# First weights in halves on two queues, an earlier place for block 1's statistics, a later one for two blocks of x

## The chip, the cores and the metric

The kernel runs on one core of a Trainium2 chip. Its engines work side by side, each through its own instructions in order: TensorE (PE, matrix products, with its weight loads as PEld), VectorE (DVE), ScalarE (ACT), GpSimd (POOL) and SyncE (SP). SP, ACT and POOL also issue DMA transfers, which sixteen DMA engines carry out. The metric is the device time of one execution in microseconds, lower is better.

## The reference

The input x has 2048 rows (tokens) of 512 columns in bfloat16. It is normalised by row, and two branches work on the result:

```python
xn = _layernorm(x, axis=-1)
# branch A: a diagonal complex state-space model along the 2048 tokens, 512 states
Bu = xn @ B_bar.T;  h[t] = Lam_bar * h[t-1] + Bu[t];  yA = 2 * (h @ C.T).real + xn * Dskip
# branch B: a gated MLP with 1792 hidden columns
yB = (silu(xn @ w1) * (xn @ w3)) @ w2
out = x + yA + yB
```

w1 and w3 are 512x1792 and w2 is 1792x512. The output is bfloat16.

## The kernel before

**Blocks.** The tokens are taken in 4 blocks of 512 (`TBLK`), each of 4 chunks of 128 rows. One tile `x_all` holds all of x, `x_blk[b]` is a block of it. For a block the kernel forms the statistics of each row (`ln_stats`, DVE), scales the rows (`xn`), transposes them (`xnT`: the 512 columns as four tiles of 128 partitions, the "depth"), multiplies with w1 and w3 (`glu`, hidden columns in 14 groups `f` of 128), forms the inputs of the state model (`bu`), scans along the tokens on DVE, and multiplies gates and states with w2 and C in seven products of sums (`y_fast`, for pairs of chunks).

**The start.** Block 0 is done by chunks, so that work can begin with the first 128 rows. x's chunks 0 and 1 are loaded in column halves, left on SP's queue and right on ACT's. Then come chunk 3 on ACT's queue (L167), chunk 2 on SP's (L168), and columns 0 to 255 and 256 to 511 of w1 and w3 (`load_w`, L169 and L170), 256 KB each, all four depths in one transfer. All of these go out before any compute instruction of SP and ACT. ACT then loads its function table (L199). PE warms up on ones (`keep_busy`, L196), transposes chunks 0 and 1 (L243) and multiplies them with the first two hidden groups in `quarter` (L619). The first `quarter` works in two depth parts: w1 with depths 0 and 1, w1 with depths 2 and 3, then w3 in the same way, eight matmuls for each of w1 and w3. The transposes of chunks 2 and 3 and the third hidden group (`quarter(0, (2,))`, columns 256 to 383) follow in PE's row. On DVE the statistics of chunks 2 and 3 stand one after the other, and behind both the scaling of chunk 2 and of chunk 3 (L224).

**Queues.** `bulk_loads` (called after the first statistics) sends the other columns of w1 and w3, x of block 1, and transposed loads of B and C over SP. `late_loads` sends w2, the row Dskip, and x of blocks 2 (by chunks) and 3 over SP. Each transfer of SP or ACT uses one of eight semaphores in turn, and the built program makes its issue wait until the transfer that used the same one eight places earlier has landed.

**The order of DVE's background work.** The order of all engines is written out by hand. Beside the products, a list `bg` of tasks is worked off: each has a cost in us, and `bg.fill()` emits tasks while DVE's planned time is less than 1.7 us (`LEAD`) ahead of PE's. `bg.flush(key)` emits all up to the last task of that key. At the start of block 0 the list holds `table_angles(2, 2)` (L376 to L380: the angles of two of the four state tiles, of which ACT makes sines and cosines later), then block 1's four statistics and the two POOL steps to its scale `rstd` (`ln1a`: L219, L220, L254, L255), then block 1's scaling and transposes (`ln1b`: L224, L247), `late_loads` and `params_w`. `ssm_tasks(0)` adds the state work of block 0 in halves: `pre` (rotation), `scans`, `post` (rotation back, whose last step is a POOL transfer that adds into `act`, L527).

**Block 2 and 3's x.** ACT forms their statistics by itself (`ln_scalar_engine`: L274, L280), emitted through `sin_step`, between evacuations of block 1's products.

Of the kernel before, what the change touches and what calls it, by code (L numbers as in the profile page):

```python
# [17 lines left out]
P = 128  # L18
# [45 lines left out]
def kernel(  # L64
# [17 lines left out]
    nc = tc.nc  # L82
# [26 lines left out]
    xv = A_x[0].rearrange("(c p) d -> p c d", p=P)  # L109
# [15 lines left out]
    w1_sb = const.tile([P, NDT, F], BF16, name="w1_sb")  # L125
    w3_sb = const.tile([P, NDT, F], BF16, name="w3_sb")
# [23 lines left out]
    x_all = xpool.tile([P, NBLK, CPB, D], BF16, name="x_blk")  # L150
    x_blk = [x_all[:, i] for i in range(NBLK)]
    w1v = B_w1.rearrange("(t p) f -> p t f", p=P)
    w3v = B_w3.rearrange("(t p) f -> p t f", p=P)

    def load_w(f0, f1, eng1=nc.sync, eng3=nc.sync):
        eng1.dma_start(out=w1_sb[:, :, f0:f1], in_=w1v[:, :, f0:f1])
        eng3.dma_start(out=w3_sb[:, :, f0:f1], in_=w3v[:, :, f0:f1])

    def load_x(b, parts=1):
        n = CPB // parts  # L160
        for i in range(0, CPB, n):
            nc.sync.dma_start(out=x_blk[b][:, i:i + n, :], in_=xv[:, b * CPB + i:b * CPB + i + n, :])

    for c in range(2):
        for eng, dsl in ((nc.sync, slice(0, D // 2)), (nc.scalar, slice(D // 2, D))):
            eng.dma_start(out=x_blk[0][:, c, dsl], in_=xv[:, c, dsl])  # L166
    nc.scalar.dma_start(out=x_blk[0][:, 3, :], in_=xv[:, 3, :])  # L167
    nc.sync.dma_start(out=x_blk[0][:, 2, :], in_=xv[:, 2, :])  # L168
    load_w(0, 2 * P)  # L169
    load_w(2 * P, 4 * P)  # L170

    def bulk_loads():
# [9 lines left out]
    def late_loads():  # L182
        nc.sync.dma_start(out=w2_sb, in_=B_w2.rearrange("(t p) d -> p t d", p=P))
        nc.sync.dma_start(out=dskip_row, in_=A_Dskip.partition_broadcast(P))
        load_x(2, 4)
        load_x(3)

# [23 lines left out]
    bg = Filler(LEAD)  # L211
# [37 lines left out]
    def ln_tasks_vector(b):  # L249
        csl = slice(b * CPB, (b + 1) * CPB)  # L250

        def finish_stats():
            vpe = lnp.tile([P, CPB], FP32, name="vpe")
            nc.gpsimd.tensor_scalar(out=vpe, in0=mv_all[:, csl, 1], scalar1=LN_EPS, scalar2=None, op0=ALU.add)  # L254
            nc.gpsimd.tensor_tensor(out=rstd_all[:, csl], in0=vpe, in1=mhalf, op=ALU.pow)  # L255

        def apply(cl):
            if cl == 0:
                ln_alloc(b)
            ln_apply(b, cl)  # L260
            ln_transpose(b, cl)

        first = [(0.85, lambda cl=cl: ln_stats(b, cl)) for cl in range(CPB)] + [(0.0, finish_stats)]
        second = [(0.4, lambda cl=cl: apply(cl)) for cl in range(CPB)]
        return first, second
# [74 lines left out]
    def sin_step(until=None):  # L340
        while sins and (until is None or until not in sins_done):
            key, fn = sins.popleft()
            fn()
            sins_done.add(key)
            if until is None:
                break
# [23 lines left out]
    def table_angles(pt, n=1):  # L370
        if pt + n > 3:
            sin_step((pt + n - 4, 0))
        slots = scratch[:, 0:2 * NPT * 2 * TBLK].bitcast(FP32).rearrange("p (h i t) -> p h i t", h=2, t=TBLK)
        ang, rnd = slots[:, 0, pt:pt + n, :], slots[:, 1, pt:pt + n, :]
        for i in range(n):
            nc.vector.tensor_scalar(out=ang[:, i, :], in0=iota_f, scalar1=turn[:, pt + i:pt + i + 1], scalar2=None,  # L376
                                    op0=ALU.mult)
        nc.vector.tensor_scalar(out=rnd, in0=ang, scalar1=MAGIC, scalar2=None, op0=ALU.add)
        nc.vector.scalar_tensor_tensor(out=ang, in0=rnd, scalar=MAGIC, in1=ang, op0=ALU.subtract, op1=ALU.subtract)
        nc.vector.tensor_scalar(out=rnd.bitcast(DT.int32), in0=ang.bitcast(DT.int32), scalar1=0x7FFFFFFF, scalar2=None,  # L380
                                op0=ALU.bitwise_and)
        for k in range(pt, pt + n):
            for i, (src, bias, scale) in enumerate(((rnd, halfpi, -TWO_PI), (ang, 0.0, -TWO_PI))):
                sins.append(((k, i), lambda k=k, i=i, src=src[:, k - pt, :], bias=bias, scale=scale: nc.scalar.activation(
                    out=tabe[:, k, i, :], in_=src, func=ACT.Sin, bias=bias, scale=scale)))
# [76 lines left out]
    def ssm_tasks(b, posts_last=False, between=(), middle=(), late=()):  # L462
# [76 lines left out]
        def add(*fns):  # L539
            for fn in fns:  # L540
                bg.add(0.0 if fn in transfers else 1.2 if fn in scans0 or fn in scans1 else 1.16, fn,
                       ("scan", b) if fn in scans0 else ("post", b) if fn in post0 else ("ssm", b))

        if b == 0:
            add(*pre0, *scans0, *post0, *pre1, *scans1, *post1)
            return
        add(*pre0)
        for t in middle:
# [32 lines left out]
    def glu(b):  # L581
# [76 lines left out]
        for f in range(f0, NFT):  # L658
            if f == AHEAD[b]:
                if b == 0:  # L660
                    ssm_tasks(0)
                if b == 2:
                    sin_step(("squares", 3, CPB - 1))
                    bg.flush(("bu", 0))
                    steps.extend(bu_fast(b, 0))
                    second = lambda: bu_fast(b, 1)
                else:
                    bu(b)
# [497 lines left out]

    ln_alloc(0)
    ln1a, ln1b = ln_tasks_vector(1)
    bg.add(3.6, lambda: table_angles(2, 2))
    for t in ln1a:  # L1170
        bg.add(*t)
    for t in ln1b:
        bg.add(*t, ("ln", 1))
    bg.add(0.0, late_loads, ("ln", 1))
    bg.add(0.2, params_w)
    gate = glu(0)
# [33 lines left out]
    def keep_ends(b):  # L1210
# [3 lines left out]
        nc.vector.tensor_copy(out=ends, in_=act(b)[:, CPB - 1].rearrange("p (h k) t -> p h k t", h=2)[:, :, NFH:NK, P - 1])  # L1214

    ssm_tasks(1, between=[(0.2, lambda: keep_ends(0))])
    gate = glu(1)
    gate()
# [6 lines left out]
    for cl, o in held:  # L1225
        nc.sync.dma_start(out=ov[:, cl, :], in_=o)
    bg.add(*difference(1))
    ssm_tasks(2, between=res_list(3), late=[(0.2, lambda: keep_ends(1)), *row_sums(2, *pairs[2]), *column_sums(3)])
    bg.first(bu_sums(2))
    gate = glu(2)  # L1230
# [52 lines left out]
```

## Time and profile before

| | us |
|---|---|
| median of 3 runs (lowest to highest) | 200.94 (200.86 to 201.03) |
| span of the profiled execution | 199.5 |
| PE busy, matmuls | 195.6 |
| DVE busy | 181.8 |
| ACT busy | 135.0 |
| POOL busy | 51.5 |

The profiled execution's span runs from its first to its last instruction; its share of the measured time outside the span is some 1.4 us if it took as long as the median. Rows of the profile name the line of the kernel, the engine, the operation, the tile written and the tiles read. A time in brackets is how long the engine stood idle before the instruction, with what ended the idle time. "SPq" and "ACTq" are DMA issues in SP's and ACT's row; a transfer's time to landing counts from the start of its issue. In the table of stretches each engine has its busy time in us and its number of instructions; the last three columns are the granted clock of TensorE, the mean busy share of the DMA engines and GB/s.

### The profile page before, as it was taken

How to read it: one execution, taken by the hardware profiler on the slowest of the kernel's cores; microseconds unless marked ns; L12 is line 12 of the kernel's file. 1: busy time of each engine (PE TensorE's matmuls, PEld its weight loads, DVE VectorE, ACT ScalarE, POOL GpSimd, SP SyncE). 2: the span in 40 equal slices, each digit the busy share in tenths (PEclk: the TensorE clock that was granted, in tenths of full speed). 3: DMA queues.
4: the chain of work that ended last, by engine and by line, in shares of the span. 5: the costliest groups of instructions: out<-in, count | busy, mean ns of one | idle time of the engine just before them, and what ended most of it. 6: DMA issues, size and time to landing. Idle time of an engine off the chain costs nothing.

```text
span 199.5 us, 3700 instructions
## 1 busy us (share of the span) xinstructions
PE 195.6 (98%) x1401; PEld 130.7 (65%) x1401; DVE 181.8 (91%) x254; ACT 135.0 (68%) x281; POOL 51.5 (26%) x75
## 2 busy tenths in 40 slices
PE   8999999999999999999999999999999999999994
PEld 2774444444444488866555468888566678888893
DVE  3689699999999999989999997999999999999972
ACT  4699897699999996968998684362588783111220
POOL 7180289700411134041202305040021303310000
PEclk9999999999999999999999999999999999999999
DMA  4999996991497054730997455838137732941111
GB/s 138 326 277 200 302 186 124 343 273 23 69 181 141 0 105 82 135 105 0 156 148 119 89 92 98 172 83 132 53 59 129 149 56 52 174 92 36 53 44 40
DMA packets 32258, 25.12 MB, mean 126 GB/s; under 512 B 16240, under 2 KB 29936, under 8 KB 32240
## 3 DMA queue, kind: packets, MB, share of 16 engines
q0 software_dynamic: 6128, 11.38, 33.5%
q1 hardware_dynamic: 25536, 13.21, 26.8%
q10 hardware_dynamic: 576, 0.30, 0.5%
q8 instruction: 11, 0.18, 0.4%
q14 instruction: 7, 0.06, 0.1%
HBM read 7.74 MB, written 2.10 MB: 49 GB/s over the span
## 4 chain that ended last, share of the span: by engine, by line
PE 95%; DMA 2%; SPq 1%; issue 0%; DVE 0%
PE gu_ps L587 34%; PE gu_ps L1054 17%; PE y_ps L1054 10%; PE gu_ps L848 7%; PE bu_ps L1054 7%; PE bu_ps L454 3%; PE y_ps L454 3%; PE y_ps L869 3%; PE y_ps L780 3%; DMA w_sb<-in_B_w_dram 2%; PE gu_ps L619 2%; PE gu_ps L780 2%; PE bu_ps L869 1%; PE bu_ps L780 1%; PE bu_ps L619 1%; SPq L166 0%
## 5 line engine op out<-in xcount | busy, mean ns | idle before, releaser
L587 PE MATMUL gu_ps<-xnT,w_sb 128*128 128x512 bf16 x312 | 69.6, 379 | 0.0
L587 PEld LDWEIGHTS <-w_sb 128*128 128x128 bf16 x312 | 30.5, 98 | 34.2
L1054 PEld LDWEIGHTS <-act 128*128 128x128 f16 x462 | 43.5, 98 | 5.4
L596 ACT ACTIVATE g<-gu_ps 128x512 bf16<-128x512 f32 x41 | 24.8, 606 | 6.0 <-PE gu_ps L587 3.6
L597 ACT ACTIVATE u<-gu_ps 128x512 bf16<-128x512 f32 x41 | 24.8, 606 | 4.5 <-PE gu_ps L587 3.7
L505 DVE TENSOR_TENSOR_SCAN u<-rho,ends,u 128x512 bf16<-128x512 f32 x16 | 20.0, 1270 | 0.0
L527 POOL DMA_DIRECT2D act<-p x7 | 9.2, 1320 | 34.0 <-DVE act L519 22.1
L1054 PE MATMUL gu_ps<-w_sb,act 128*128 128x256 bf16 (+3 forms) x126 | 16.0, 267 | 0.0
L848 PE MATMUL gu_ps<-xnT,w_sb 128*128 128x512 bf16 x64 | 15.9, 379 | 0.0
L604 DVE TENSOR_TENSOR act<-g,u 128x1024 f16<-128x1024 bf16 x21 | 14.2, 679 | 0.4 <-ACT u L597 0.4
L860 ACT ACTIVATE g<-gu_ps 128x512 bf16<-128x512 f32 x14 | 8.4, 599 | 5.4 <-PE gu_ps L848 5.0
L454 PEld LDWEIGHTS <-bt 128*128 128x128 bf16 x64 | 6.3, 98 | 7.5
L1077 ACT ACTIVATE x_blk<-gu_ps 128x256 f32<-128x256 f32 (+1 forms) x9 | 3.3, 368 | 10.6 <-PE gu_ps L1054 10.6
L1054 PE MATMUL bu_ps<-w_sb,act 128*128 128x256 bf16 (+3 forms) x84 | 10.4, 264 | 0.0
L1054 PE MATMUL gu_ps<-ct,act 128*128 128x256 f16 (+1 forms) x72 | 10.4, 267 | 0.0
L848 PEld LDWEIGHTS <-w_sb 128*128 128x128 bf16 x64 | 6.3, 98 | 4.8
L505 DVE TENSOR_TENSOR_SCAN u<-rho,u 128x512 bf16<-128x512 f32 x8 | 9.2, 1206 | 0.0
L1054 PEld LDWEIGHTS <-x_blk 128*128 128x128 f16 x88 | 8.6, 98 | 1.0
L1054 PEld LDWEIGHTS <-tw 128*128 128x128 f16 x88 | 8.6, 98 | 1.0
L513 DVE TENSOR_TENSOR p<-u,tabe 128x2048 f16<-128x2048 bf16 (+1 forms) x8 | 8.7, 1085 | 0.1
L519 DVE TENSOR_TENSOR act<-u,tabe 128x2048 f16<-128x2048 bf16 (+1 forms) x8 | 8.7, 1083 | 0.0
L488 DVE TENSOR_TENSOR u<-u,tabe 128x2048 bf16<-128x2048 bf16 x7 | 8.5, 1219 | 0.1
(203 smaller groups left out, 392.5 us busy)
## 6 DMA issues: line engine op xcount, KB each, us to landing
act<-p POOLq DMA_DIRECT2D x6, 512.0 KB, 6.1
xn<-x_blk POOLq DMA_DIRECT2D x4, 512.0 KB, 5.5
out_dram<-xn SPq DMA_DIRECT2D x15, 128.0 KB, 1.7
w_sb<-in_B_w_dram SPq DMA_DIRECT2D x1, 1792.0 KB, 8.2
act<-act POOLq DMA_DIRECT2D x5, 352.0 KB, 4.6
w_sb<-in_B_w_dram SPq DMA_DIRECT2D x2, 768.0 KB, 6.4
u<-p POOLq DMA_DIRECT2D x3, 512.0 KB, 5.1
w_sb<-in_B_w_dram SPq DMA_DIRECT2D x4, 256.0 KB, 4.9
```

What stands on the lines that cost most here:

```text
L454: nc.tensor.matmul(out=ps, lhsT=bt[:, ri, dt, pt * P:(pt + 1) * P], rhs=xnT_blk[b][:, dt, :], start=(dt == 0), stop=(dt == NDT - 1))
L505: nc.vector.tensor_tensor_scan(out=v, data0=rho[:, pt:pt + 1].to_broadcast([P, TBLK]), data1=v, initial=init, op0=ALU.mult, op1=ALU.add)
L513: nc.vector.tensor_tensor(out=by_state(st["p16"][:, csl]), in0=by_chunk(st["g"][:, :, ::-1, tsl]), in1=by_chunk(tabe[:, psl, 2:0:-1, tsl]) ...
L519: nc.vector.tensor_tensor(out=by_state(act_state(b, hf)[:, csl]), in0=by_chunk(st["g"][:, :, :, tsl]), in1=by_chunk(tabe[:, psl, 0:1, tsl] ...
L527: gp.dma_start(out=a, in_=p16, accum_op=ALU.add)
L587: nc.tensor.matmul(out=ps[:, tsl], lhsT=w[:, dt, f * P:(f + 1) * P], rhs=xnT[:, dt, tsl], start=(dt == 0), stop=(dt == NDT - 1))
L596: nc.scalar.activation(out=g16[:, f % 2, :], in_=g_ps, func=ACT.Silu)
L597: nc.scalar.activation(out=u16[:, f % 2, :], in_=u_ps, func=ACT.Copy)
L604: nc.vector.tensor_tensor(out=act_gates(b, f - 1), in0=split(g16), in1=split(u16), op=ALU.mult)
L780: nc.tensor.matmul(out=out[:, h * TH:(h + 1) * TH], lhsT=left[:, h, k, :], rhs=right[:, k, :], start=(start and h == 0 and k == 0), stop=( ...
L848: nc.tensor.matmul(out=ps, lhsT=w[:, dt, f * P:(f + 1) * P], rhs=xnT[:, dt, :], start=(dt == 0), stop=(dt == NDT - 1))
L1054: nc.tensor.matmul(out=out, lhsT=left[:, k, :], rhs=right[k][:, cols], start=(start and k == 0), stop=(k == NK - 1), skip_group_check=True)
```

## The change

Three things are moved. (1) The first weights (columns 0 to 255) are sent in four transfers of 128 KB, by depth halves: depths 0 and 1 of w1 and w3 on SP's queue, depths 2 and 3 on ACT's. x's chunk 2 goes out on SP behind the first half of w1, and chunk 3, so far on ACT, goes out on SP behind the first half of w3. (2) Block 1's four statistics with their POOL steps stand ahead of `table_angles(2, 2)` in the list. (3) The loads of x of blocks 2 and 3 leave `late_loads` and become a task of their own behind block 0's state work. A POOL memset of one column of these blocks stands ahead of them, and since the loads overwrite that column they wait for it.

```diff
-    nc.scalar.dma_start(out=x_blk[0][:, 3, :], in_=xv[:, 3, :])
-    nc.sync.dma_start(out=x_blk[0][:, 2, :], in_=xv[:, 2, :])
-    load_w(0, 2 * P)
+    w_parts = [(w_sb, wv, i) for w_sb, wv in ((w1_sb, w1v), (w3_sb, w3v)) for i in (0, 2)]
+    for (w_sb, wv, i), eng in zip(w_parts, (nc.sync, nc.scalar, nc.sync, nc.scalar)):
+        eng.dma_start(out=w_sb[:, i:i + 2, 0:2 * P], in_=wv[:, i:i + 2, 0:2 * P])
+        if w_sb is w1_sb and i == 2:
+            nc.sync.dma_start(out=x_blk[0][:, 2, :], in_=xv[:, 2, :])
+    nc.sync.dma_start(out=x_blk[0][:, 3, :], in_=xv[:, 3, :])
     load_w(2 * P, 4 * P)
...
     def late_loads():
         nc.sync.dma_start(out=w2_sb, in_=B_w2.rearrange("(t p) d -> p t d", p=P))
         nc.sync.dma_start(out=dskip_row, in_=A_Dskip.partition_broadcast(P))
+
+    def last_x_loads():
+        nc.gpsimd.memset(x_all[:, 2:4, 0, 0:1], 0.0)
         load_x(2, 4)
         load_x(3)
...
         if b == 0:
             add(*pre0, *scans0, *post0, *pre1, *scans1, *post1)
+            bg.add(0.0, last_x_loads)
             return
...
     ln1a, ln1b = ln_tasks_vector(1)
-    bg.add(3.6, lambda: table_angles(2, 2))
     for t in ln1a:
         bg.add(*t)
+    bg.add(3.6, lambda: table_angles(2, 2))
     for t in ln1b:
         bg.add(*t, ("ln", 1))
```

## The prediction

> **What bounds the kernel now.** I read first the shares by engine and the 40 slices, then the chain that ended last, then the first 14 us of that chain and of the timeline, then the DMA throughput there.
>
> ```profile
> PE 195.6 (98%) x1401; PEld 130.7 (65%) x1401; DVE 181.8 (91%) x254; ACT 135.0 (68%) x281; POOL 51.5 (26%) x75
> ...
> PE 95%; DMA 2%; SPq 1%; issue 0%; DVE 0%
> ```
>
> TensorE carries 95% of the chain. From 9.3 us on it has one matmul after another to 196.6 us, 0.216 us for each of 512 columns, and the list of waits names none of PE's later than the quarters of block 0. So time can be won only by starting this row of matmuls sooner, and is lost by any hole put into it. The one piece of the chain that isn't PE is the 2% of DMA: the first weights. Here are the first pieces of the chain in order (start, length, what), and rows of the timeline:
>
> ```profile
> 2.58 4.53 DMA w_sb<-in_B_w_dram
> ...
> 7.16 1.51 PE gu_ps L619 x24
> 8.67 0.11 PE y_ps L315
> 8.78 0.33 PE y_ps L243 x4
> 9.11 0.58 PE bu_ps L619 x8
> 9.69 0.22 PE y_ps L243 x4
> 9.92 0.45 PE bu_ps L619 x8
> ```
> ```profile
> 6.27 0.45 PEld L619 LDWEIGHTS <-w_sb 128*128 128x128 bf16 x8 [0.18 <-DMA w_sb<-in_B_w_dram]
> ...
> 7.15 1.34 PEld L619 LDWEIGHTS <-w_sb 128*128 128x128 bf16 x24 [0.44 <-DMA w_sb<-in_B_w_dram]
> ```
>
> Three waits for weights stand in PE's row. It is free for `quarter` at 6.09 and starts at 6.27, when w1 (columns 0 to 255) lands: 0.17. Eight matmuls later it waits for w3: 0.43. And the eight of `quarter(0, (2,))` at 9.11 take 0.58 where the same eight take 0.45 at 9.92: 0.13 for w3 of columns 256 to 511, which was issued at 3.69 and took 5.6, so landed at 9.29. Together 0.73 us. That third wait matters most, since it is met last.
>
> ```profile
> 2.00:3.00 1.00, 1.00 (x4) 0.44 (x3) 0.00 (x0) 0.87 (x1) 1.00 (x3) 1.00 1.15 272
> 3.00:4.00 1.00, 1.00 (x4) 0.29 (x2) 0.89 (x3) 0.41 (x1) 0.93 (x3) 1.00 0.47 154
> 4.00:5.00 1.00, 0.92 (x3) 0.15 (x1) 0.96 (x4) 0.85 (x4) 0.61 (x3) 1.00 0.82 250
> 5.00:6.00 1.00, 0.91 (x11) 0.60 (x12) 0.89 (x4) 0.92 (x4) 0.00 (x0) 1.00 1.13 329
> 6.00:7.00 1.00, 0.88 (x12) 0.53 (x10) 0.96 (x3) 0.77 (x3) 0.00 (x0) 1.00 1.17 309
> ```
>
> The last two columns are the DMA engines' busy share and GB/s. From 3 to 5 us the 16 engines stand half idle though four transfers are queued: what was issued did not reach them fast enough. The granted clock, third from the end, is 1.00 throughout and plays no part.
>
> **The change part by part.** The sum is made against the profiled execution, span 199.5; the median is 200.94, so 1.4 us lie outside the span, taken as unchanged.
>
> *First weights.* Nothing is added in bytes: 1.5 MB (block 0's x and columns 0 to 511 of w1 and w3) still go out ahead of the bulk loads. Two 256 KB issues become four of 128 KB, two of them on ACT's queue, which loses chunk 3 of x to SP. Issues by the rows (0.42 to 0.51 each): SP has upper w1 at 1.64 (w1 whole: 2.11), chunk 2 at 2.1, upper w3 (built to wait for the left half of chunk 0, issued 0.73, landing after 2.1, seen by DVE at 3.08) at 3.1, chunk 3 at 3.55 (was 1.65 on ACT), then columns 256 to 511 at 4.0 and 4.5 (were 3.13, 3.69), the next weights at 5.0 (4.88), x of block 1 some 0.1 later than 6.05. ACT has lower w1 at 1.65 and lower w3 at 2.1.
>
> *First two waits.* w1 is now the first 256 KB behind the 256 KB of chunks 0 and 1, and it was the third 256 KB (landing 6.2); chunks 2 and 3 had that place and landed at 5.3 to 5.65. By that row w1 is there by 5.7, before the 6.09 at which PE is free and xnT's first part (written 5.41 to 5.74) is there. w3 is wanted after w1's eight matmuls, at 6.09 + 0.45 = 6.54; its lower half is ahead of where w1 stood, its upper half is ahead of chunk 3 alone. The fourth 256 KB landed at 7.1 before; a share of the half-idle stretch must be recovered for it to be there at 6.54. Bounds for the two waits: 0 to 0.60 gained, and no loss, since PE can't need them sooner. Then `quarter(1)` follows at 6.99, when xnT of chunk 1 (ACT L244, to 6.89) is just there; the row by 8.89 stands up to 0.60 earlier, at 8.29.
>
> *Third wait.* There PE wants w1, then at 8.51 w3, of columns 256 to 511. w3 is still the last of the same 1.5 MB. If the engines carry no more than before, it lands at 9.29 as before, and whatever was gained ahead is handed back: 0. If the stretch from 3 to 5 us ran at the 319 GB/s of 5 to 7, the missing 165 and 69 KB come in, 0.73 us sooner, 8.56: nearly all 0.73. Which? With 256 KB behind each queue by 2.6 us the stretch is most like 2 to 3 us, where both queues held equal loads: 272 GB/s. Then 3 to 4 us gives 118 KB more and 4 to 5 us some 50 to 69, about 170 KB in all, 0.53 us at 319. I take 0.53: landing 8.76. The SP's later issue (4.5) is no limit: before, this transfer waited 5.6 us in the queue, and from 4.5 it has 4.2 left.
>
> The Trainium skill, DMA: Bandwidth & Descriptors, section "Issuing engines are not separate DMA queues", speaks against this: all issuers share the same 16 engines, and spreading saves the sequencer's issue time only. By it the third wait would end at 9.29 and the gain would be 0; by the row above, in which the engines are half idle with work issued, it is 0.53.
>
> *ACT.* Its third issue (0.45) becomes two, so the table load (1.28 from 2.13) goes to 2.6, ending at 3.9; its first work starts at 4.09. If an issue of 256 pieces costs 0.6 instead, it ends at 4.1 and all is 0.05 late. I take 0, bounds 0 to 0.1 lost.
>
> *Chunk 3 of x.* DVE takes its statistics at 6.54, and the scaling of chunk 2 (7.34) stands behind them.
>
> ```profile
> 6.54 0.66 DVE L219 BATCH_NORM_STATS2 stats<-x_blk 128x6 f32<-128x512 bf16 x1
> 7.23 0.18 DVE L220 BATCH_NORM_AGGREGATE mv_all<-stats 128x2 f32<-128x6 f32 x1
> 7.34 0.41 DVE L224 TENSOR_SCALAR xn<-x_blk,mv_all,rstd_all 128x512 bf16<-128x512 bf16 x1
> ```
>
> It is now the end of the first 1 MB, where w3 stood: landing 7.1 at the old rate, 6.6 with the 0.53. PE wants chunk 2's scaled rows at 8.1 (8.71 less 0.6), and they are ready at 7.75: 0.35 of cover. At 6.6 nothing is lost, at 7.1 0.2. Bounds 0 to 0.25; I take 0.
>
> *Statistics of block 1 ahead of the last angles.* The same instructions in another order: four pairs of 0.66 and 0.18 move from 18.2-22.1 to about 14.2-17.7, the angles (3.6) from 14.7 to about 18.4. POOL's 1.4 us for rstd and DVE's wait of 1.47 for it fall under the angles, so DVE is about 1 us ahead after 25 us. x of block 1 lands at 6.05 + 7.7 = 13.75; a later landing would hold DVE, with the gate of L604 behind it and ACT's buffers behind that, but it would need over 1 us. The angles must be there for ACT's table at 25.66; they are by 22.5. On SP the four transposes at 26.27 stand behind the ct transposes anyhow. No PE wait names DVE after 6 us, so this is 0 (bounds 0 and 0.1 lost).
>
> *x of blocks 2 and 3.* Five SP issues leave 33.5 to 36.5 and wait for a POOL memset (0.10 by L208) behind the second act transfer (50.95, 1.28), so they go out from 52.4. Behind SP's wait stand only block 2's transposes (77.05), which need ACT's norm. ACT reads block 2 from 61.9, a chunk each 1.9 us; with the 8.1 us that these loads took beside w2, chunks land from 60.5 to 62.5. Cover 1.4 us and more. They now share the engines with two POOL accumulations (5.5 and 6.9 us); the first feeds DVE L1000 at 59.50 and lands at 56.4. One megabyte at 330 GB/s is 3.1 us if served wholly first: 59.5, just in time, and PE wants the sums only at 70. I take 0, bounds 0 to 0.2 lost.
>
> **Sum:** 0.53 gained. 200.94 - 0.53 = 200.4.
>
> **The rivals.**
> - *The bytes decide.* DMA carries no more than before; PE is ahead by 0.6 at 8.3 and waits 0.6 to 0.75 for the last w3. For it: order alone is changed, and between 3 and 5 us the cause of the idle engines isn't shown. Against: the load of the queues was lopsided (640 KB on SP, 128 KB on ACT). Gain 0 to 0.35: 200.6 to 200.95.
> - *All recovered:* 0.73, with 0.1 if the parameters' transpose (0.11 at 8.67) closes up: 200.1 to 200.2.
> - *Slower: chunk 3 is late.* Fifth on SP, behind a wait for a landing. If it lands after 7.5 (6.54 and the 0.96 by which chunk 2's rows lead PE at 8.71), PE starts those transposes later than before, and the delay runs through the whole row. At 3.55 plus the 5.2 us that the transfer issued at 3.13 took, it lands at 8.75 and costs 1.25: 202.2. Landing at 7.9 costs 0.4. Against: in front of it lie only 896 KB, in front of that one 1 MB.
>
> **How the numbers follow.** Gain near 0.53 or above (0.4 to 0.85): 0.56. Bytes decide (loss 0.1 to gain 0.4): 0.30. Late chunk 3 (or ACT, or block 2's loads) by over 0.4: 0.14. 0.2% is 0.40 us, about what a measurement of this kernel can tell from no change. The forecast is on the edge of it, so faster 0.56, same 0.30, slower 0.14. The range runs from all recovered (200.1) to nothing gained with 0.15 lost beside it (201.1), leaving the slower case and a little below out. The faster case alone: 200.1 to 200.55.
>
> **What would show it.** Right: no wait for weights before the first eight of `quarter`, the next at about 6.55; DMA above 0.8 from 3 to 5 us; eight matmuls at about 8.3 with a wait of 0.2 to 0.3 inside; the first 512-column matmul at 12.35 (12.88); DVE's 1.47 wait gone; PE without holes to the end. Wrong: a wait of 0.6 or more at 8.5 (bytes), a DVE wait ahead of the fourth statistics longer than 0.4 (chunk 3), a PE wait near 62 us (block 2). An early DMA stretch no better than 154 and 250 GB/s would make the forecast wrong.

## The result: slower by 1.2%, and the profile after

The changed kernel takes 203.5 us (203.07 to 203.65), the kernel before on the same chip 200.9 us. The ratio is 1.012, with a 95% interval of 1.0104 to 1.0135. The forecast was 200.4, with a range to 201.1: wrong in sign. The profiled execution after took 203.52 us, its span is 201.75 us where that of before is 199.53: 2.22 us more, and the next lines say where they are.

First the page of the kernel after: its head, the busy times, and the shares of the chain that ended last.

```profile
span 201.8 us, 3706 instructions
...
PE 195.2 (97%) x1401; PEld 130.5 (65%) x1401; DVE 181.8 (90%) x254; ACT 135.1 (67%) x281; POOL 47.2 (23%) x76
...
PE 69%; DVE 17%; DMA 7%; issue 4%; ACT 0%; POOL 0%; POOLq 0%; DVEq 0%
```

PE is as busy as before (195.2 us for 195.6), but it carries 69% of the chain, not 95%. In 17% the chain runs through DVE, and DMA has 7%. So somewhere in the middle PE waits for DVE, which itself waits for a transfer. The list of waits from 26 to 190 us (PE) and from 50 to 80 us (DVE) of the kernel after names both (in all, times, longest):

```profile
PE bu_ps L1061 <- DVE act L1103: 1.8, 1, 1.8
...
DVE x_blk L1007 <- DMA xn<-x_blk: 3.1, 2, 2.1
```

The chain of the same kernel leads from the one to the other (start, length, what). The pieces left out are twelve DVE instructions and some steps of 0.1 us or less:

```profile
57.38 8.76 DMA xn<-x_blk
...
66.26 0.89 DVE x_blk L1007
...
76.84 0.81 DVE act L1103
...
77.69 1.38 PE bu_ps L1061 x11
```

And the timeline of the kernel after, from 50 to 78 us, shows who is meant:

```profile
51.44 0.62 POOL L190 MEMSET x_blk<- 128x2 bf16 x1
51.79 1.11 POOL L944 DMA_DIRECT2D xn<-x_blk  x1
52.09 5.02 SPq L162 DMA_DIRECT2D x_blk<-in_A_x_dram  x5
57.38 0.86 POOL L944 DMA_DIRECT2D xn<-x_blk  x1 [4.48 <-DVE xn L940]
60.26 0.89 DVE L1007 TENSOR_TENSOR x_blk<-act 128x1408 f16<-128x1408 f16 x1 [0.96 <-DMA xn<-x_blk]
66.26 0.89 DVE L1007 TENSOR_TENSOR x_blk<-x_blk,act 128x1408 f16<-128x1408 f16 x1 [2.12 <-DMA xn<-x_blk]
76.75 0.88 DVE L1103 TENSOR_TENSOR act<-act,x_blk 128x1408 f16<-128x1408 f16 x1
```

The same three DVE instructions in the timeline of the kernel before, without any wait:

```profile
59.50 0.88 DVE L1000 TENSOR_TENSOR x_blk<-act 128x1408 f16<-128x1408 f16 x1
...
63.29 0.88 DVE L1000 TENSOR_TENSOR x_blk<-x_blk,act 128x1408 f16<-128x1408 f16 x1
...
73.77 0.88 DVE L1096 TENSOR_TENSOR act<-act,x_blk 128x1408 f16<-128x1408 f16 x1
```

The two transfers `xn<-x_blk` are the residual: `res_list` adds x into `xn` by an accumulating transfer of POOL, 512 KB for each block (L944 after, L937 before). `row_sums` (L1007 after, L1000 before) then writes two sums of `act`, `s3` and `s2`. `sum_homes` gives it as room for them the x tiles of blocks 0 and 1, just the tiles which those transfers still read. So the first sum waits for the first residual, the second for the second. Before, these landed at 52.08 + 6.9 = 59.0 and 57.67 + 5.1 = 62.8 us, both 0.5 us before DVE came. After, they run beside five plain loads, which SP issues from 52.09, and land at 51.79 + 8.4 = 60.2 and 57.38 + 8.76 = 66.1. DVE stands idle for 0.96 and 2.12 us, has no spare time behind that, and comes to the sum that PE wants 2.98 us later than before (76.75 against 73.77). It had led PE by some 1.1 us there: the sum was done at 74.65 before, and PE's first matmul that reads it started at 75.86 (after, PE starts 0.06 us behind the end of the sum). So PE loses 1.9 us.

Why the residuals are that late is seen in the stretches of 2 us (the last two columns are the share of the DMA engines and GB/s), first of the kernel before, then of the kernel after:

```profile
54.00:56.00 2.00, 2.00 (x11) 0.88 (x9) 1.97 (x3) 1.97 (x4) 0.00 (x0) 1.00 1.23 179
56.00:58.00 2.00, 2.00 (x11) 0.89 (x10) 2.00 (x4) 1.94 (x5) 0.33 (x1) 1.00 1.10 211
...
62.00:64.00 2.00, 2.00 (x11) 0.88 (x9) 2.00 (x4) 1.97 (x6) 0.00 (x0) 1.00 1.00 182
```
```profile
56.00:58.00 2.00, 2.00 (x11) 0.94 (x10) 2.00 (x3) 1.93 (x5) 0.62 (x1) 1.00 1.17 242
...
60.00:62.00 2.00, 2.00 (x12) 0.88 (x9) 1.75 (x3) 1.97 (x5) 0.56 (x1) 1.00 1.12 353
...
64.00:66.00 2.00, 2.00 (x11) 0.92 (x10) 0.13 (x1) 1.97 (x7) 0.00 (x0) 1.00 0.96 182
```

Before, only accumulating transfers run here, and in these stretches they already keep the engines busy (1.00 and above) while they move 179 to 211 GB/s. Only from 58 to 62 us was there a little room beside them (shares of 0.74 and 0.88). After, the loads' bytes came on top (242 and 353 GB/s in the rows shown), and the accumulations went on after the last load had landed at 63.8, at 182 GB/s.

Now the start, where the gain was expected. The stretches of the kernel after from 2 to 7 us:

```profile
2.00:3.00 1.00, 1.00 (x4) 0.44 (x3) 0.06 (x1) 0.33 (x1) 1.00 (x3) 1.00 0.83 196
3.00:4.00 1.00, 1.00 (x5) 0.34 (x3) 0.81 (x2) 0.99 (x2) 0.93 (x3) 1.00 0.85 236
4.00:5.00 1.00, 0.50 (x3) 0.00 (x1) 0.91 (x3) 0.67 (x3) 0.60 (x3) 1.00 1.07 313
5.00:6.00 1.00, 0.74 (x8) 0.46 (x8) 0.89 (x4) 0.92 (x4) 0.00 (x0) 1.00 0.93 209
6.00:7.00 1.00, 0.87 (x13) 0.67 (x12) 0.76 (x2) 0.77 (x3) 0.00 (x0) 1.00 0.81 234
```

The hole from 3 to 5 us is filled as forecast (236 and 313 GB/s for 154 and 250), but 2 to 3 fell from 272 to 196, and 5 to 7 from 319 to 221. Over all five the mean is 238 GB/s, where it was 263. Pieces of the chain and rows of the timeline of the kernel after show what PE got of it:

```profile
2.93 4.06 DMA w_sb<-in_B_w_dram
...
7.04 1.51 PE gu_ps L626 x24
...
9.04 0.56 PE bu_ps L626 x8
```
```profile
7.03 1.34 PEld L626 LDWEIGHTS <-w_sb 128*128 128x128 bf16 x24 [0.33 <-DMA w_sb<-in_B_w_dram]
...
7.38 0.69 DVE L225 BATCH_NORM_STATS2 stats<-x_blk 128x6 f32<-128x512 bf16 x1 [0.58 <-DMA x_blk<-in_A_x_dram]
...
12.79 1.46 PE L594 MATMUL gu_ps<-xnT,w_sb 128*128 128x512 bf16 x6
```

The wait for w1 is gone. The wait for w3 (its upper half was issued at 2.93) is 0.33 for 0.44, and the third wait is still there: 0.56 for eight matmuls that take 0.45 elsewhere. The first matmul of 512 columns starts at 12.79, not 12.88: 0.09 us won where 0.53 was forecast.

The third piece is at the end. From the start of the last matmul to the end of the span it is 2.98 us before and 3.36 after. SP's own waits from 196 us on say why, in the kernel before and then in the kernel after (in all, times, longest):

```profile
SPq L1278 <- DMA out_dram<-xn: 1.0, 3, 0.5
```
```profile
SPq L1285 <- DMA out_dram<-xn: 1.3, 2, 1.1
```

The program ends with SP going through the eight transfer semaphores, one after another in a fixed order. Before, the last three stores were counted on the last three of that row (landings at 198.10, 198.31 and 198.62 us), so that SP had passed all others while it waited. The change has two more transfers, which turns the assignment on by two. After, the last stores fall on the last, the first and the second of the row (199.92, 200.16 and 200.47), so SP first waits 1.1 us and still has six semaphores to go through behind the last landing. From the last landing to the end it is 0.91 us before, 1.28 after.

The sum: 1.92 (PE's wait) + 0.38 (end) - 0.09 (start) = 2.21 us of the 2.22. PE's wait is taken from the starts of its matmuls, 75.66 and 77.69, which otherwise follow each other by 0.11; the list of waits goes by modelled ends and has 1.8. The medians differ by 2.6. The rest is most likely a late start in the profiled execution of before, as the other profiles below suggest.

### The profile page after: what moved, and what is told of

It is laid out like the page before. It is cut to its first block, busy times and chain, and to the rows that moved or that the text cites. A ratio compares the mean times of both kernels' runs of the same rounds, so it can differ in the third digit from the quotient of the medians.

```text
span 201.8 us, 3706 instructions
## 1 busy us (share of the span) xinstructions
PE 195.2 (97%) x1401; PEld 130.5 (65%) x1401; DVE 181.8 (90%) x254; ACT 135.1 (67%) x281; POOL 47.2 (23%) x76
## 4 chain that ended last, share of the span: by engine, by line
PE 69%; DVE 17%; DMA 7%; issue 4%; ACT 0%; POOL 0%; POOLq 0%; DVEq 0%
PE gu_ps L1061 17%; PE gu_ps L594 16%; PE y_ps L1061 8%; PE gu_ps L855 7%; PE bu_ps L1061 5%; DVE u L511 4%; DMA xn<-x_blk 4%; PE y_ps L876 3%; PE y_ps L787 3%; DVE act L611 3%; DVE u L494 2%; DVE p L490 2%; DMA w_sb<-in_B_w_dram 2%; PE gu_ps L626 2%; PE gu_ps L787 2%
## 5 line engine op out<-in xcount | busy, mean ns | idle before, releaser
L225 DVE BATCH_NORM_STATS2 stats<-x_blk 128x6 f32<-128x512 bf16 x8 | 5.4, 680 | 3.7 <-DMA x_blk<-in_A_x_dram 3.7
```

## The experiments

Theory A: the late loads of x slow the residual transfers, DVE waits for these, and PE for DVE; nothing else in the change costs over 0.5 us. Rivals: the memset or its place in POOL's row does it (B), or the new order of weights or of statistics disturbs DVE (C).

**One part at a time.** The loads alone on the kernel before:

```diff
     def late_loads():
         ...
+
+    def last_x_loads():
+        nc.gpsimd.memset(x_all[:, 2:4, 0, 0:1], 0.0)
         load_x(2, 4)
         load_x(3)
...
             add(*pre0, *scans0, *post0, *pre1, *scans1, *post1)
+            bg.add(0.0, last_x_loads)
```

> The kernel before with part 3 alone (x of blocks 2 and 3 loaded behind block 0's state work). Theory, traffic: the loads run beside POOL's two accumulations of x into xn, these land late, DVE's first sums (L1000, which write over the x tiles that those transfers read) wait for them, and PE waits about 1.9 us for DVE near 75 us. So 1.9 us over before, 202.8, with a wait of DVE on the transfer xn<-x_blk of 2 us or more, and no change of the tail. Rival, first weights: the loss hangs on the weights' part as well; then this run is within 0.4 us of before.

203.21 us, ratio 1.0118 (1.0074 to 1.0161). The waits of this run, for PE and for DVE, are those of the kernel after:

```profile
PE bu_ps L1058 <- DVE act L1100: 1.9, 1, 1.9
...
DVE x_blk L1004 <- DMA xn<-x_blk: 3.0, 2, 2.0
```

The part alone gives most of the loss: 2.1 us between its medians, where the whole change has 2.6. The other two parts without it (parts 1 and 2 of the diff shown above):

> The changed kernel without part 3: weights in halves and statistics ahead. Theory: no PE wait near 75 us; the start gains 0.1 us or less; the end loses 0.4 us, because two transfers more turn the rotation of the eight semaphores so that the last three landings are met early in the final row of waits instead of last. 201.2, 0.3 over before. Rival (the tail belongs to the late loads): 200.8, 0.1 under before.

201.79 us, ratio 1.0039 (1.0022 to 1.0056): no wait near 75 us, but no gain either; 0.7 us are lost where 0.3 was expected. The weights alone, and the statistics alone:

> The kernel before with part 1 alone. Theory: as without part 3, 201.2: first 512-column matmul at about 12.8, last matmul 0.1 us earlier than before, tail 0.4 us longer. Rival (the halves do bring half a us, and it is lost later): last matmul 0.4 us or more earlier.

> The kernel before with part 2 alone. All theories: DVE about 1 us ahead after 25 us, no PE wait added or taken away, 200.9 within 0.2 us of before.

The weights give 201.65, 1.0037 (1.0021 to 1.0053): by themselves a small loss, 0.56 us where 0.3 was expected. The statistics give 201.03, 0.9999 (0.9987 to 1.0012): nothing. The large loss isn't theirs, so C falls, and the weights have to be looked at by themselves. What the statistics were to save has only moved, from a wait for POOL to one for ACT. DVE's waits name it, in the kernel before and then in the kernel after (in all, times, longest):

```profile
DVE xn L224 <- POOL rstd_all L255: 1.5, 1, 1.5
```
```profile
DVE p L490 <- ACT u L462: 1.5, 1, 1.5
```

The run of the statistics alone has the same wait for ACT, 1.46 us. The instruction behind it (`p<-u,tabe`) starts there at 25.39, before at 26.02. So DVE is 0.63 us ahead and not about 1, and 0.40 of this is the earlier start of that profile's row of matmuls (12.48 for 12.88).

**The memset alone, and the loads earlier.** For B, the kernel before with a memset of a spare tile in the same place and no load moved; for A, the same loads and memset half of block 0's state work earlier, so that SP issues them at 39.02 us, when no residual is under way:

```diff
+    spare_col = const.tile([P, 2], BF16, name="spare_col")
...
             add(*pre0, *scans0, *post0, *pre1, *scans1, *post1)
+            bg.add(0.0, lambda: nc.gpsimd.memset(spare_col, 0.0))
```
```diff
-            add(*pre0, *scans0, *post0, *pre1, *scans1, *post1)
+            add(*pre0, *scans0, *post0)
+            bg.add(0.0, last_x_loads)
+            add(*pre1, *scans1, *post1)
```

> The kernel before with a POOL memset of a spare tile at the place of part 3's memset; the loads stay early. Theory, traffic: POOL's later issue by 0.1 to 0.6 us is nothing by itself, no PE wait near 75 us, within 0.2 us of before. Rival, POOL's order: the memset ahead of the accumulations makes them late, PE waits 1 to 2 us near 75 us and the time is 202 to 203.

> The kernel before with the loads of x of blocks 2 and 3 and their memset behind the first half's last step of block 0 (POOL's transfer at 37 us) instead of the second half's. They then run from about 39 to 45 us, where the engines are else idle until 52. Theory, traffic: no wait of DVE for xn<-x_blk, no PE wait near 75 us, within 0.2 us of before. Rival, the memset and SP's wait on POOL cost by themselves, wherever they stand: 1 us or more over before.

200.88 us, 0.9998 (0.9983 to 1.0013), and 200.81 us, 0.9991 (0.9977 to 1.0004). Both stand where the kernel before stands. In the second the residuals, asked for by their tile, take the times of before again (min/median/max to landing), where the kernel after shows 8.4/8.6/8.8:

```profile
DMA to landing us min/median/max: 5.1/6.1/7.1
```

So neither the memset nor moving the loads costs anything that these intervals show. What costs is what the loads share the engines with. B falls. The kernel before has the same collision at another place: there the loads of x run beside POOL's transfer `act<-p` of 37.56 us, which takes 9.1 us to land, and with the loads of x gone from there (the kernel after) the same transfer takes 5.8. No list of waits names it, so nobody pays.

**Half the bytes.** Only block 3's x, 512 KB, is sent late; block 2 stays where it was:

```diff
         load_x(2, 4)
+
+    def last_x_loads():
+        nc.gpsimd.memset(x_all[:, 3:4, 0, 0:1], 0.0)
         load_x(3)
...
             add(*pre0, *scans0, *post0, *pre1, *scans1, *post1)
+            bg.add(0.0, last_x_loads)
```

> The kernel before with only block 3's x (512 KB) behind block 0's state work; block 2's x stays with w2. Theory, traffic: half the bytes beside the accumulations, so DVE waits for xn<-x_blk about half as long as with both blocks (3.0 us there), 1 to 1.8 us in all. DVE has about 1 us to give before PE feels it (3.0 us of waiting cost PE 1.9 to 2.0), so PE waits 0 to 0.7 us near 75 us: 201.0 to 201.7. Rival, any late load costs the same whatever its size: PE waits 1.9 us, 202.9.

201.73 us, 1.0038 (1.002 to 1.0056). Its waits, for PE and for DVE:

```profile
PE bu_ps L1058 <- DVE act L1100: 0.5, 1, 0.5
...
DVE x_blk L1004 <- DMA xn<-x_blk: 1.7, 1, 1.7
```

DVE loses 1.67 us, where all the bytes cost it 3.08: about half for half the bytes. In both cases the 1.1 us by which DVE leads PE come off, so PE's matmul starts 0.61 us late (at 76.08, the one before it at 75.36) where it was 1.92. A stands: fewer bytes cost less. But the loss isn't simply in proportion to the bytes. The first residual lands 9.1 us after its issue, later than with all the bytes (8.4), and the whole stall is there; the second takes 6.9, and DVE doesn't wait for it. What counts is which residual the loads run beside.

**The end.** To test the turning of the semaphores, the kernel before with one transfer more (block 3's x in two pieces, at the old place), and parts 1 and 2 of the change with block 2's x in two pieces instead of four, so that the count of transfers is again that of before:

```diff
         load_x(2, 4)
-        load_x(3)
+        load_x(3, 2)
```
```diff
-        load_x(2, 4)
+        load_x(2, 2)
```

> The kernel before with the load of block 3 in two transfers of 256 KB, one transfer more in all. Theory, rotation: the last three stores move on by one semaphore, the last of them to the first in the final row of waits, so that about seven waits of 0.06 us follow its landing: from the last matmul to the end 3.35 to 3.4 us in place of 2.98, and 0.4 us over before. Rival (the longer tail comes from the weights' part in another way, or by chance): 2.98 and no change.

> The changed kernel without part 3 and with block 2's x in two transfers in place of four, so that the count of transfers is that of before again. Theory, rotation: from the last matmul to the end 2.98 us again, 0.4 us less than with parts 1 and 2 alone; what is left against before is the start, within 0.3 us. Rival: 3.35 as with parts 1 and 2.

One transfer more: 201.47 us, 1.0022 (1.0008 to 1.0036), the end takes 3.42 us for 2.98. The count as before: 201.29, 1.0018 (0.9996 to 1.0041), and the end takes 2.98 again. SP's waits at the end, of the first and then of the second of these:

```profile
SPq L1278 <- DMA out_dram<-xn: 1.4, 1, 1.4
```
```profile
SPq L1281 <- DMA out_dram<-xn: 1.0, 3, 0.5
```

A transfer that holds nothing up where it stands, at 35 us, costs 0.4 us at the end, by its number.

**The weights.** With the count as before, 0.36 us of loss are left (interval -0.1 to 0.8, so not clear of noise) where a gain of 0.53 was forecast. Two experiments, both made on this kernel. In the first, upper w3 goes out ahead of chunk 2, so that its issue no longer waits for a landing:

```diff
-        if w_sb is w1_sb and i == 2:
-            nc.sync.dma_start(out=x_blk[0][:, 2, :], in_=xv[:, 2, :])
+    nc.sync.dma_start(out=x_blk[0][:, 2, :], in_=xv[:, 2, :])
     nc.sync.dma_start(out=x_blk[0][:, 3, :], in_=xv[:, 3, :])
```

> The changed kernel without part 3, with the count of transfers of before, and with upper w3 issued ahead of chunk 2, so that it needs no wait for chunk 0's landing and is issued at 2.1 us, not 2.9. Theory, bytes: upper w3 lands near 5.7 in place of 6.9 and the wait of PE for it goes, but the last of the same 1.5 MB lands at 8.7 to 9.2 as ever, and chunks 2 and 3 land later (about 6.4 and 7.3), so what is won at 6.5 is given back by 9.3: first 512-column matmul at 12.5 to 12.8, time within 0.3 us of before. Rival, issue: upper w3's late issue was what took the gain of part 1 away; then the first 512-column matmul is at 12.0 to 12.2 and the time 200.5 or less.

201.89 us, 1.004 (1.0024 to 1.0056). PE's wait for w3 is gone, its 32 matmuls run in one piece from 6.26. Rows of its timeline show what came instead:

```profile
6.72 0.70 DVE L221 BATCH_NORM_STATS2 stats<-x_blk 128x6 f32<-128x512 bf16 x1 [1.03 <-DMA x_blk<-in_A_x_dram]
...
8.79 0.40 PE L245 MATMUL y_ps<-ident,xn 128*128 128x128 bf16 x4 [0.29 <-DVE xn L226]
```

Chunk 2 is late, DVE's statistics wait 1.03 us for it, and PE waits for the scaled rows instead of for w3. The first matmul of 512 columns starts at 12.92, and the time is 0.9 us over before, both worse than either expectation. So the wait for a landing in SP's row isn't what eats the gain; the bytes are late in another place.

In the second, chunk 3 goes out on ACT's queue and not on SP's, which was meant to bring all of SP's later issues forward:

```diff
-    nc.sync.dma_start(out=x_blk[0][:, 3, :], in_=xv[:, 3, :])
+    nc.scalar.dma_start(out=x_blk[0][:, 3, :], in_=xv[:, 3, :])
```

> Parts 1 and 2 of the change, block 2's x in two transfers, with chunk 3 of block 0's x on ACT's queue (behind lower w3) and no longer on SP's. It asks why the DMA engines carry less from 5 to 7 us with the weights in halves (212 to 243 GB/s in every profile so far) than with the old order (304 to 320). If it is because SP's issues of columns 256 to 511 and the bulk loads come 0.45 us later, one issue less on SP brings them forward by that: the stretch is back near 300 GB/s, chunk 3 lands by 6.8, the last w3 lands by 8.7, and the first 512-column matmul starts at 12.4 to 12.5; time 200.9 to 201.1. If it is the mixture of transfers itself, the stretch stays at 210 to 245 GB/s, the last w3 lands at 9.0 to 9.3 and the first 512-column matmul starts at 12.6 to 12.9; time 201.2 to 201.5, and 0.1 to 0.4 more if ACT, with three issues of 0.45 ahead of its table load, is late for block 0 (table load until 4.4 where it was 3.95).

201.97 us, 1.0056 (1.004 to 1.0073). Of the expectation one half came and the other didn't. Two stretches, and then three pieces of the chain of this run:

```profile
5.00:6.00 1.00, 0.43 (x5) 0.29 (x6) 0.79 (x3) 0.83 (x5) 0.00 (x0) 1.00 1.05 300
6.00:7.00 1.00, 1.00 (x18) 0.86 (x15) 0.97 (x3) 0.80 (x3) 0.00 (x0) 1.00 1.08 313
```
```profile
2.76 4.44 DMA w_sb<-in_B_w_dram
...
7.25 1.51 PE gu_ps L622 x24
...
9.20 0.45 PE bu_ps L622 x8
```

The engines carry 300 and 313 GB/s again: five profiles with chunk 3 on SP have 212 to 243 GB/s over these 2 us, this one 307. The last w3 lands at 8.60, and the third wait is gone (0.45 for eight matmuls). But this can't be put down to earlier issues of SP. Columns 256 to 511 went out at 3.93 and 4.35, only 0.12 us earlier than in the kernel after (4.05 and 4.47), and the run with the count as before, with 243 GB/s, has them earlier still (3.81 and 4.29); the next weights went out at 5.49, later than in both (5.09 and 4.91). What differs is chunk 3 itself, which was issued at 2.93 for 3.30 to 3.49, and on the other queue. These two aren't told apart, and why the stretch from 5 to 7 us falls stays open. The start is no earlier either (12.83). ACT's table load goes from 3.31 to 4.59, its first instruction to 4.60, and block 0's first transposes start at 5.57 where they started at 5.25 in the kernel after. And upper w3 still lands at 7.20: fifteen of its sixteen parts were there by 6.40 and one at 7.20, 0.25 us after PE wanted it. The Trainium skill, DMA: Bandwidth & Descriptors, section "Why a DMA increments its semaphore by 16 and not by 1", has the rule behind this: a DMA runs on up to 16 engines that finish independently, and the semaphore counts them. A small transfer lands with its slowest part.

**How far a start can be read.** The first matmul of 512 columns, in all profiles with the old order of weights, started at 12.17, 12.23, 12.48, 12.48, 12.65, 12.72 and, in the profile before, 12.88 us: mean 12.52. In those with halves as in the change it was 12.51, 12.67, 12.75 and 12.79: mean 12.68. The two groups overlap, so that no difference between them is shown. The profile on which the forecast was built is the latest start of its kind. Against the mean, the change's start (12.79) is 0.27 late and not 0.09 early, and with this estimate 1.92 + 0.38 + 0.27 = 2.6 us comes to the difference of the medians. The hole from 3 to 5 us was unusual too: 202 GB/s in the profile before, 220 to 280 in the other six, 258 to 279 with halves.

No version that beats both kernels came out of this: the best (the loads of x at 39 us, 200.81) is within the uncertainty of the kernel before.

## Why the prediction was wrong

- **What bounds the kernel:** right, but for the end of the program. One row of matmuls from 9 us on, which loses time by holes in it; the change put one hole in.
- **x of blocks 2 and 3:** this step failed, and most of the loss is here (1.92 of 2.21 us). It was costed at 0 with bounds to 0.2. It named the right neighbours (two accumulations by POOL, DVE L1000 at 59.50) and then said that the first transfer feeds L1000 and lands at 56.4. That is the landing of `act<-p`, which L1000 reads but which isn't the last that it needs. What releases L1000 is the residual `xn<-x_blk`, through the tile that L1000 writes, and it lands at 59.0: 0.5 us of cover, not 3. The bound of 3.1 us, "if served wholly first", was near the truth (the residuals landed 1.2 and 3.4 us later), but it was held against the wrong landing. And "PE wants the sums only at 70" counted the distance of one sum from PE, where DVE's lead counts: 1.1 us at the sum that PE wanted near 75.8. Later instructions of DVE inherit each stall in full, since its waits list shows no gap in which to catch up.
- **The check for it** was a PE wait near 62 us, because block 2 was watched for late x. The loads were in time for block 2, as the forecast said; the hole came 13 us later, by way of blocks 0 and 1.
- **First weights:** forecast 0.53, measured no gain, and a small loss that is not clear of noise once the end is taken off. The row at 6.1 us was right (no wait for w1). In the profile after, the engines were filled from 3 to 5 us, as forecast. But the step took it that the other stretches would keep their rates: 2 to 3 us fell to 196 GB/s and 5 to 7 us to 221, and the last w3 landed at 9.16 (forecast 8.76; before 9.25, which the sum has as 9.29). And the third wait it meant to shorten was that of one execution: none of the six other profiles with the old order has it (0.45 us for the eight matmuls), and their last w3 landed at 8.20 to 8.78; with halves as in the change it landed at 8.71 to 9.16. So the term of 0.53 had little to draw on. Its working slips as well: at the 272 GB/s that it takes, 4 to 5 us gives 22 KB more and not 50 to 69, so 0.44 us. That SP's later issue (4.5) is no limit isn't refuted: issued at 4.29 and 4.35, the last w3 landed at 8.71 and 8.60. The rival "the bytes decide" had the size (0 to 0.35), but the bytes per us changed, and why is open. The rule weighed there, that issuers share the 16 engines and spreading saves issue time only, gave the right sum for this part: 0. That chunk 3 on ACT's queue went with 307 GB/s in place of 212 to 243 it doesn't settle, since its issue was earlier as well.
- **Chunk 3 late:** landed at 7.35, DVE waited 0.58, PE nothing. Within the bounds, and the cover of 0.35 to 0.96 held; in the run of the weights alone the chain goes through this chunk, at a cost of some 0.1. The slower rival was the wrong one.
- **ACT's table load** (2.67 to 3.95, first work at 3.97): 0, as forecast.
- **Statistics of block 1:** 0, as forecast (0.9999); but the reason was wrong in part: DVE's wait of 1.47 is gone, a wait of 1.46 for ACT came in its place, and DVE is not about 1 us ahead after 25 us.
- **Not in the forecast at all:** the end, 0.38 us. The prediction counted the issues of SP and ACT and had the turning semaphores in view at the start, but not what their turn does to the last stores.
- **The base:** the profile before held the latest start of seven of its order; by the mean of the starts 0.36 of the 0.73 us of waits that the sum drew on were not there to be won in a usual execution. It fits that 1.4 us outside the span was too little: all runs that have both their time and their span on record show 1.7 to 1.9.

## What to carry to other kernels

Before a load is moved into a stretch, look at the busy share of the DMA engines there, not at their GB/s: here accumulating transfers had them at 1.0 and above at 179 to 211 GB/s, and a megabyte more beside these made DVE wait for 3.1 us. For each transfer that will share the stretch, find all that it releases, also whoever writes over a tile that it reads, and compare its landing with the start of that instruction; the cover is that much, plus the lead of the waiting engine over the one that it feeds, and all its stalls together draw on this lead. And a change in the number of transfers is a change in itself, by what it does to the end.

## What the runs showed of the hardware

- The two residuals, accumulating transfers of 512 KB each, took 5.1 to 7.1 us with only other accumulating transfers beside them, at a DMA share of 1.00 to 1.23 and 179 to 211 GB/s in the fullest stretches, and 8.4 to 8.8 us beside 1 MB of plain loads. The transfer `act<-p` at 37 us, of the same size, took 9.1 us beside these loads and 5.8 without them.
- One transfer more (at 35 us) made the end of the program 0.44 us longer, and two more (among the first weights) 0.38, because SP passes the eight semaphores in fixed order; with the count of before, the end was that of before.
- The start of programs that are alike up to there differs by 0.7 us from execution to execution (12.17 to 12.88), and it goes with the DMA throughput from 3 to 5 us: 202, 220 and 231 GB/s where it started at 12.88, 12.72 and 12.65, and 263 to 280 where it started at 12.17 to 12.48. Why the throughput differs was not tried.
